# A routed two-layer expert kernel: the first routing round makes its differences ahead on GpSimd, and the first expert begins with halves of its tokens

## The chip, the core and the metric

The kernel is one program on one core of a Trainium2 chip. The metric is the device time of one execution in microseconds (us); a kernel is judged by the median of several executions. Five engines work side by side, each taking its own instructions strictly in their order: PE (TensorE, matmul), DVE (VectorE), ACT (ScalarE), POOL (GpSimd) and SP (here only a queue of DMA issues).

## The reference

```python
def _attn_ref(q, k, v):            # retention: 8 batches, 8 heads, 576 positions, head size 64
    scores = np.matmul(q, k.transpose(0, 1, 3, 2)) / np.sqrt(D_)
    return np.matmul(scores * Dmat, v)          # Dmat: gamma_h ** (i - j), lower triangle
def _moe_ref(x, w_in, w_out):      # 4608 tokens, 512 -> 2048 -> 512
    h = x @ w_in
    return (h - np.tanh(h)) @ w_out
def _moe2_ref(x, w_gate, w1, w2):  # 8 experts of 1024, each takes exactly 576 tokens
    order = np.argsort(-(x @ w_gate).flatten())
    for idx in order:              # best (token, expert) pairs first
        tok, e = idx // E, idx % E
        if assigned[tok] >= 0 or counts[e] >= cap: continue
        assigned[tok] = e; counts[e] += 1
    for e in range(E):
        out[assigned == e] = np.maximum(x[assigned == e] @ w1[e], 0.0) @ w2[e]
```

## The kernel before

Two parts follow each other. In the first (up to about 1043 us) retention and the first pair of layers are computed, and with them the table L of 4608 x 8 gate logits. The change does not touch this part. The second part, `phase_c`, routes tokens and runs the eight experts.

Routing goes in rounds r = 0 to 7; each round fills one expert. All 4608 tokens stand as 128 partitions x 36 columns. A round looks for the threshold of a key: twice ("half" 0 and 1, the upper and the lower 16 bits) it takes three steps of 32, 32 and 64 candidate thresholds. A step compares all keys with all its candidates on DVE (`cmp`, 128 x 36 x 32 or 64), counts with matmuls of the comparison against the proposal table P (`pa`), scales the counts (`ca`), sums them with two small matmuls (`pd`), and finds on DVE the last candidate that still fits (`dm`, `tr`, `pi`). Then come the expert's number `ei` (which lets SP load its weights), running positions, the tables A and R (R in two parts, one of them by ACT), a matmul of the two (`pi`), two small DVE instructions (`im`, `ix`), a last small matmul, and `idx`, the list of the expert's tokens. From `idx` GpSimd gathers 5 tiles of 128 tokens (`xg`).

Only round 0 has nothing to run beside: PE has no other work then. It is "fast": for step 2 GpSimd makes the differences key - threshold ahead (`D`), so that step 2 is one DVE tensor_scalar on D with the two earlier results as per-partition scalars, and not a tensor_tensor.

The rounds 1 to 7, the weight splits (`split_w`: every weight tile is split by ACT into a high part and by POOL into a low part) and the token tiles (`tokens`: 4 PE transposes `tp`, an ACT copy `xh`, a DVE subtraction `xl`) are three Python generators. `experts(r)` writes the matmuls of expert r and after each one or two of them calls `tick`, which advances a clock and lets the generators write their next piece. So the instruction order on every engine is set by that clock and by the numbers behind `yield`, not by readiness on the chip.

An expert has two stages. Stage 1: eight blocks f of 24 matmuls (12 products for each half u of 288 tokens) into two PSUM tiles `ff` of a pool of four; ACT then writes `hh` (relu), and DVE writes `hl` with three instructions that read the same two PSUM tiles. Block f + 2 uses the tiles of block f, so its first matmuls wait until DVE has made `hl` of block f. Stage 2: five output tiles t in the order 0, 4, 1, 2, 3, of 24 matmuls (16 for t = 4, whose parts DVE adds to `o`). The code writes `hl` of block f after the sixth matmul of the next block:

```python
if late and j == 5:
    late.pop()()
```

Of the kernel before, what the change touches and what calls it, by code (L numbers as in the profile page):

```python
# [9 lines left out]
F32 = mybir.dt.float32  # L10
F32R = mybir.dt.float32r
# [16 lines left out]
NCOL = NTOK // 128  # L28
# [687 lines left out]
def phase_c(tc, ctx, w1, w2, rtf, rti, rth, rtb, x2d, L, out):  # L716
# [89 lines left out]
    def route(r):  # L806
# [29 lines left out]
        if r < E - 1:  # L836
# [6 lines left out]
            for half in range(2):  # L843
# [7 lines left out]
                for s, (shift, J) in enumerate(STEPS):  # L851
                    if s == 0:
# [3 lines left out]
                        if fast:  # L856

                            if not half:
                                src = rt([128, NCOL], F32, "hf")
                                nc.gpsimd.tensor_copy(out=src, in_=hi)  # L860
                            D = fp.tile([128, KC, CAP], F32R, tag="xl", name="D", bufs=2)
                            D = D.rearrange("p k t -> p (k t)")[:, :NCOL * 64].bitcast(F32)
                            D = D.rearrange("p (c j) -> p c j", c=NCOL)
# [95 lines left out]
        X72 = X.rearrange("p a c -> p (a c)")  # L959
        nc.tensor.matmul(pt[:, 72:], B["ones"], X72, start=True, stop=True)  # L960
        nc.tensor.matmul(pt[:, :72], B["tri"], X72, start=True, stop=True)
        if r < E - 1:
            se = rt([128, E], F32, "se")
            V.tensor_scalar(se, SB["w8"], mx, None, op0=OP.is_equal)
            V.scalar_tensor_tensor(epen, se, -2 * BIG, epen, op0=OP.mult, op1=OP.add)
            VN[r + 1] = rt([128, NCOL, E], F32, "v")
            V.tensor_tensor(VN[r + 1], L, bc(epen, 1, NCOL), op=OP.min)
        pos = SB["pos"]
        vd = rt([128, 72], F32, "vd")
        pb = rt([128, NCOL], F32, "pb")  # L970
# [23 lines left out]
        if r < E - 1:  # L994

            V.tensor_tensor(SB["hs"], gg[:, :, 0], vd[:, NCOL:], op=OP.add)
            V.scalar_tensor_tensor(tpen, SB["hs"], -2 * BIG, tpen, op0=OP.mult, op1=OP.add)
            V.tensor_tensor(m8, m8, gg[:, :, 0], op=OP.mult)
            V.tensor_tensor(own, own, m8, op=OP.add)
            V.tensor_tensor(rem, rem, nn[:, 0, :], op=OP.subtract)  # L1000
# [10 lines left out]
        if r < E - 1:  # L1011
# [10 lines left out]
    EV, WS, W1, W2, XT, first_done = {}, {}, {}, {}, {}, {}  # L1022

    def load_w1(r):
        EV[r] = nc.sync.value_load(EI[r][:1, :1], min_val=0, max_val=E - 1)
# [29 lines left out]
    def tokens(r):  # L1055
# [17 lines left out]
        for t in range(5):  # L1073
# [4 lines left out]
            h, l = (x[:, :, 128 * t:128 * t + n] for x in (xh, xl))  # L1078
            nc.scalar.activation(h, tp[:, :, :n], AF.Copy)
            V.tensor_tensor(l, tp[:, :, :n], h.bitcast(F32), op=OP.subtract)  # L1080
            yield 1.3
        XT[r] = xh, xl

# [16 lines left out]
                    th_[0] = clock[0] + d * (YS[len(IDX) > 1] if th_ is threads[0] else YS[0])  # L1100

    def experts(r):
        while r not in XT:
            tick(0.2)
        xh, xl = XT.pop(r)
        idx = IDX[r]
        H, late = [], []
        load_w2(r, 0)
        load_w2(r, 1)
        for f in range(8):  # L1110
            load_w2(r, f + 2)
            ps = [psF.tile([128, 512], F32, tag="ff", name="ff")[:, :288] for _ in range(2)]
            while f not in W1:
                tick(0.2)
            w1h, w1l = W1.pop(f)
            prods = [(w, xh, k) for k in range(KC) for w in (w1h, w1l)] + [(w1h, xl, k) for k in range(KC)]
            seq = [(i, u) for i in range(12) for u in range(2)]
            if r == 0 and f == 0:

                seq = [(i, u) for a, b in ((0, 8), (8, 12)) for u in range(2) for i in range(a, b)]  # L1120
            for j, (i, u) in enumerate(seq):
                w, x, k = prods[i]
# [3 lines left out]
                if late and j == 5:  # L1126
                    late.pop()()

            hh = fp.tile([128, CAP + 64], F32R, tag=f"hh{f}", name="hh")
            hl = fp.tile([128, CAP - 64], F32R, tag=f"hl{f}", name="hl")  # L1130
            for u in range(2):
                nc.scalar.activation(hh[:, 288 * u:288 * u + 288], ps[u], AF.Relu)

            def low(ps=ps, hh=hh, hl=hl):
                for a, b, o in ((0, 288, hl[:, :288]), (288, 512, hl[:, 288:]), (512, 576, hh[:, 576:])):
                    V.scalar_tensor_tensor(o, ps[a // 288][:, a % 288:a % 288 + b - a], 0.0, hh[:, a:b].bitcast(F32),  # L1136
                                           op0=OP.max, op1=OP.subtract)
            late.append(low)
            H.append((hh, hl))
            split_w(r, 2, f)  # L1140
            first_done[r] = f == 7
        late.pop()()
        for t in (0, 4, 1, 2, 3):
# [35 lines left out]
    for _ in range(WARM2):  # L1179
        nc.tensor.matmul(warm, B["ones"], tb[:, 256:768], start=True, stop=True)  # L1180

    threads[2][0] = 2.0
    while 0 not in XT:
        tick(0.2)
    for r in range(E):
        experts(r)

# [80 lines left out]
```

## Time and profile before

| what | value |
|---|---|
| times of three runs | 1585.72, 1584.21, 1582.7 us |
| median | 1584.21 us |
| the profiled execution's own time | 1585.81 us, of which the profile's span is 1584.0 us |
| PE busy | 1490.9 us, 94% of the span |
| DVE, ACT, POOL busy | 1131.5, 760.2 and 562.6 us |
| TensorE's granted clock, mean over the span | 0.97 of full speed (2.4 GHz; the lower level is 1.2 GHz) |

Times in the profile count from the start of the span. A matmul's duration is modelled and overlaps the next one's, so pitches (start to start) are used where matmuls follow each other. Brackets at the end of a row tell how long the engine was idle before the instruction, and what it waited for.

### The profile page before, as it was taken

What the parts mean: (1) busy time and instruction counts of PE and PEld (TensorE: products, weight loads), DVE (VectorE), ACT (ScalarE), POOL (GpSimd) and SP (SyncE); (2) the same over time, 40 slices, a digit from 0 to 9 for tenths busy, and PEclk for the clock granted to TensorE, in tenths of its full rate; (3) what the DMA queues carried; (4) which work ended last, traced back from release to release, by engine and by line L of the source; (5) the groups of instructions that cost most, each with busy time, mean ns of one, the idle gap of its engine ahead of it and who ended that gap; (6) DMA issues with size and microseconds to landing.
All of it is one profiled execution on the core that took longest, in us unless ns stands there. A gap on an engine that the chain in (4) does not pass through costs nothing.

```text
span 1584.0 us, 25586 instructions
## 1 busy us (share of the span) xinstructions
PE 1490.9 (94%) x9180; PEld 1291.2 (82%) x9180; DVE 1131.5 (71%) x2772; ACT 760.2 (48%) x1585; POOL 562.6 (36%) x490
## 2 busy tenths in 40 slices
PE   6889998999999999999999999955999999999997
PEld 4678887888888888888888888844887887887996
DVE  6999974878777877777877777867767767766210
ACT  4657873554656454646455556512323323323421
POOL 3546551222213121312221313234545545356542
PEclk7989998999999999999999999976999999999999
DMA  7522220211111111111111100013324324325310
GB/s 255 163 98 80 78 111 21 82 66 41 58 43 49 53 41 61 41 61 41 61 41 42 60 23 20 1 36 112 111 88 137 120 78 136 121 77 190 101 64 30
DMA packets 48607, 122.37 MB, mean 77 GB/s; under 512 B 6624, under 2 KB 13408, under 8 KB 48224
## 3 DMA queue, kind: packets, MB, share of 16 engines
q1 hardware_dynamic: 41184, 99.80, 19.1%
q0 software_dynamic: 6144, 19.93, 3.9%
q8 instruction: 72, 1.18, 0.3%
q10 hardware_dynamic: 1152, 1.02, 0.2%
q14 instruction: 55, 0.45, 0.1%
HBM read 101.85 MB, written 18.87 MB: 76 GB/s over the span
## 4 chain that ended last, share of the span: by engine, by line
PE 76%; DVE 13%; issue 4%; DMA 2%; ACT 2%; POOL 2%; SPq 0%; POOLq 0%; DVEq 0%; ACTq 0%
PE h L394 22%; PE x L457 22%; PE ff L1154 11%; PE ff L1123 10%; PE ps L292 2%; PE ps L339 2%; PE ps L285 2%; PE ps L344 2%; DVE t L418 1%; DVE work L204 1%; PE tp L1077 1%; DVE t L424 1%; DVE work L203 1%; DVE t L420 1%; DVE work L222 1%
## 5 line engine op out<-in xcount | busy, mean ns | idle before, releaser
L438 POOL TENSOR_TENSOR gl<-t,gh 128x384 fp32r<-128x384 f32 x192 | 204.2, 1064 | 664.7 <-ACT gh L435 606.1
L394 PE MATMUL h<-xh,w0h 128*128 128x384 f32 x704 | 239.9, 341 | 3.4 <-DVE t L424 3.3
L404 ACT ACTIVATE S<-h 128x384 f32<-128x384 f32 x192 | 93.7, 488 | 305.7 <-PE h L394 305.4
L394 PE MATMUL h<-xh,w0l 128*128 128x384 f32 x704 | 239.8, 341 | 0.0
L457 PE MATMUL x<-w1h,gh 128*128 128x512 f32 x576 | 235.8, 409 | 2.4 <-ACT gh L435 2.4
L418 DVE SCALAR_TENSOR_TENSOR t<-t,S 128x384 f32<-128x384 f32 x192 | 115.0, 599 | 162.2 <-ACT t L407 161.2
L457 PE MATMUL x<-w1l,gh 128*128 128x512 f32 x576 | 229.5, 398 | 0.0
L457 PE MATMUL x<-w1h,gl 128*128 128x512 f32 x576 | 218.9, 398 | 0.4 <-POOL gl L438 0.4
L498 DVE SCALAR_TENSOR_TENSOR junk<-x2r,wg 128x512 f32<-128x512 f32 x240 | 164.5, 685 | 4.7
L394 PE MATMUL h<-xl,w0h 128*128 128x384 f32 x704 | 153.1, 339 | 0.0
L394 PEld LDWEIGHTS h<-xh,w0h 128*128 128x128 f32 x704 | 133.2, 189 | 13.2 <-DVE t L424 5.5
L1040 POOL TENSOR_TENSOR w2l<-ws,w2h 128x512 fp32r<-128x512 f32 x64 | 82.6, 1292 | 162.9 <-ACT w2h L1039 160.3
L394 PEld LDWEIGHTS h<-xh,w0l 128*128 128x128 f32 x704 | 133.0, 189 | 7.3
L457 PEld LDWEIGHTS x<-w1h,gl 128*128 128x128 f32 x576 | 108.9, 189 | 27.7 <-POOL gl L438 1.5
L1154 PE MATMUL ff<-w2h,hh 128*128 128x512 f32 x320 | 127.6, 399 | 3.0 <-DVE hl L1136 2.0
L424 DVE COPY_PREDICATED t<-m,h 128x384 f32<-128x384 uint16 x192 | 114.8, 598 | 20.4 <-ACT m L413 0.7
L1154 PE MATMUL ff<-w2l,hh 128*128 128x512 f32 (+1 forms) x320 | 127.3, 398 | 0.6 <-POOL w2l L1040 0.6
L407 ACT ACTIVATE t<-S,bias 128x384 f32<-128x384 f32 x192 | 118.3, 616 | 19.0 <-POOL gl L438 3.0
L394 PEld LDWEIGHTS h<-xl,w0h 128*128 128x128 f32 x704 | 126.9, 188 | 0.0
L457 PEld LDWEIGHTS x<-w1h,gh 128*128 128x128 f32 x576 | 109.4, 190 | 20.9 <-ACT gh L435 3.0
L457 PEld LDWEIGHTS x<-w1l,gh 128*128 128x128 f32 x576 | 109.4, 190 | 18.0
L1123 PE MATMUL ff<-xh,w1h 128*128 128x288 f32 x512 | 116.1, 305 | 6.2 <-DVE hl L1136 5.4
(206 smaller groups left out, 3031.3 us busy)
## 6 DMA issues: line engine op xcount, KB each, us to landing
ws<-in_w SPq DMA_DIRECT2D x128, 256.0 KB, 3.6
ain<-in_qkv SPq DMA_DIRECT2D x36, 768.0 KB, 4.2
wst<-in_wio SPq DMA_DIRECT2D x32, 512.0 KB, 3.7
x2d<-x2r SPq DMA_DIRECT2D x33, 256.0 KB, 2.0
w1h<-in_qkv SPq DMA_DIRECT2D x12, 192.0 KB, 3.3
w1l<-in_qkv SPq DMA_DIRECT2D x12, 192.0 KB, 3.4
w0h<-in_qkv SPq DMA_DIRECT2D x12, 192.0 KB, 3.8
w0l<-in_qkv SPq DMA_DIRECT2D x12, 192.0 KB, 4.1
```

The source lines that it names most:

```text
L285: nc.tensor.matmul(PSA[k][a][:, chunk(c)], kt[r, chunk(c)], q[r, chunk(c)], start=True, stop=True)
L394: nc.tensor.matmul(h[:, :TB], w[0][f][:, hp, :], x, start=i == 0, stop=i == 11)
L404: nc.scalar.activation(S, h, AF.Square, scale=KSC)
L407: nc.scalar.activation(AT[s][2], AT[s][1], AF.Square, bias=bias[:, 0:1])
L418: nc.vector.scalar_tensor_tensor(t, t, PA - PB * PB / 4, S, op0=OP.add, op1=OP.mult)
L424: nc.vector.copy_predicated(t, m.bitcast(U16), h)
L438: nc.gpsimd.tensor_tensor(G[s][1], TT.pop(s), G[s][0].bitcast(F32), op=OP.subtract)
L457: nc.tensor.matmul(X2[n][i], g[:, i * 128:i * 128 + 128], w, start=(f == 0 and g is gh and w is wh), stop=(f == NF - 1 and g is gl))
L498: nc.vector.scalar_tensor_tensor(j, r, 1.0, wg[e // 4][:, e % 4, :], op0=OP.mult, op1=OP.mult, accum_out=L[:, c, e:e + 1])
L1040: nc.gpsimd.tensor_tensor(l, s, h.bitcast(F32), op=OP.subtract)
L1123: nc.tensor.matmul(ps[u], w[:, k, :], x[:, k, 288 * u:288 * u + 288], start=i == 0, stop=i == 11)
L1154: nc.tensor.matmul(o, h, w, start=f == 0 and i == 0, stop=f == 7 and i == len(prods) - 1, skip_group_check=t == 4)
```

## The change

Four things are changed, all around round 0 and expert 0.

1. In each half of round 0 GpSimd makes two differences, 32 candidates for step 1 (in the buffers of the token tiles `xh`) and then 64 for step 2 (as before). Step 1 becomes one tensor_scalar on the first of them, in place of a small tensor_scalar (the thresholds) and a tensor_tensor.
2. The next round's values (`se`, `epen`, `v`) are written behind the tables in round 0, and the state update and `best(1)` behind `idx`.
3. Expert 0 starts when three of its five token tiles are there. Its blocks 0 and 1 go together: first the token half u = 0 of both, then u = 1 of both, each with its own ACT relu. Both `hl` come after the sixth matmul of block 2.
4. The routing generator begins at clock 2.0 like the token generator, and the loop that first completed all five tiles is gone.

```diff
-                            D = fp.tile([128, KC, CAP], F32R, tag="xl", name="D", bufs=2)
...
-                            nc.gpsimd.tensor_tensor(D, bc(src, 2, 64), bc(F["s2"], 1, NCOL), op=OP.subtract)
+                            D = []
+                            for i, (n, tag) in enumerate(((32, "xh"), (64, "xl"))):
+                                d = fp.tile([128, KC, CAP], F32R, tag=tag, name="D", bufs=2)
+                                d = d.rearrange("p k t -> p (k t)")[:, :NCOL * n].bitcast(F32)
+                                D.append(d.rearrange("p (c j) -> p c j", c=NCOL))
+                                nc.gpsimd.tensor_tensor(D[i], bc(src, 2, n), bc(F[f"s{i + 1}"], 1, NCOL), op=OP.subtract)
...
+                    elif s == 1 and fast:
+                        cmp_ = rt([128, NCOL, J], BF16, "cmp32")
+                        V.tensor_scalar(cmp_, D[0], pi, None, op0=OP.is_ge)
+                        T = pi
                     elif s == 2 and fast:
                         cmp_ = rt([128, NCOL, J], BF16, "cmp64")
-                        V.tensor_scalar(cmp_, D, T, pi, op0=OP.subtract, op1=OP.is_ge)
+                        V.tensor_scalar(cmp_, D[1], T, pi, op0=OP.subtract, op1=OP.is_ge)
...
+        def values():
...
+                V.tensor_scalar(se, SB["w8"], mx, None, op0=OP.is_equal)
+                V.scalar_tensor_tensor(epen, se, -2 * BIG, epen, op0=OP.mult, op1=OP.add)
+                VN[r + 1] = rt([128, NCOL, E], F32, "v")
+                V.tensor_tensor(VN[r + 1], L, bc(epen, 1, NCOL), op=OP.min)
...
+        if r:
+            values()
...
+        (state if r else values)()
...
-        if r < E - 1:
+        if 0 < r < E - 1:
             best(r + 1)
...
         IDX[r] = idx
+        if r == 0:
+            state()
+            best(1)
...
+            XP[r] = xh, xl, t + 1
...
-        while r not in XT:
+
+        while (XP.get(r, (0, 0, 0))[2] < 3) if r == 0 else r not in XT:
             tick(0.2)
...
+        for fs in ([(0, 1)] if r == 0 else [(0,), (1,)]) + [(f,) for f in range(2, 8)]:
+            load_w2(r, fs[0] + 2)
+            seq = []
+            for f in fs:
...
+                seq += [(u if len(fs) > 1 else 0, f, i, u, ps, *p) for i, p in enumerate(prods) for u in range(2)]
...
+            seq.sort(key=lambda p: p[0])
+            for j, (part, f, i, u, ps, w, x, k) in enumerate(seq):
+                while part and r not in XT:
+                    tick(0.2)
                 nc.tensor.matmul(ps[u], w[:, k, :], x[:, k, 288 * u:288 * u + 288], start=i == 0, stop=i == 11)
...
+                while late and j == 5:
+                    late.pop(0)()
...
-    threads[2][0] = 2.0
-    while 0 not in XT:
-        tick(0.2)
+    threads[0][0] = threads[2][0] = 2.0
```

The change moves instructions on all engines; three places are shown here as the compiled order has them.

On DVE, early in stage 1 of expert 0, before the change: the 64-candidate comparison of round 1 (`cmp64`, in two pieces) and behind it `hl` of block 0, which reads the tiles ff_10873 and ff_10874.

```order
L886 COPY T_10856<-st_10365 128x1
L890 TENSOR_TENSOR cmp64_10854<-hi_10706,st_10365 128x36x32
L1080 TENSOR_TENSOR xl2_10776<-tp_10859,xh2_10775 128x4x64
L903 TENSOR_TENSOR ca_10914<-rt_10895,tf_10357 128x32
L1136 SCALAR_TENSOR_TENSOR hl_10921<-ff_10873,hh_10920 128x288
L1136 SCALAR_TENSOR_TENSOR hl_10921<-ff_10874,hh_10920 128x224
L1136 SCALAR_TENSOR_TENSOR hh_10920<-ff_10874,hh_10920 128x64
```

The same place with the change; ff_10832 and ff_10833 are the PSUM tiles of block 0, and block 2 is to use them again.

```order
L892 COPY T_10911<-st_10365 128x1
L896 TENSOR_TENSOR cmp64_10909<-hi_10708,st_10365 128x36x32 x2
L1160 SCALAR_TENSOR_TENSOR hl_10835<-ff_10832,hh_10834 128x288
L1160 SCALAR_TENSOR_TENSOR hl_10835<-ff_10833,hh_10834 128x224
L1160 SCALAR_TENSOR_TENSOR hh_10834<-ff_10833,hh_10834 128x64
L1160 SCALAR_TENSOR_TENSOR hl_10839<-ff_10836,hh_10838 128x288
```

Before, the small matmuls on PE (L914) that lead to this comparison stood ahead of the first matmul of block 0, so 48 matmuls lay between them and block 2. Now they (L920) stand after the 30th matmul of blocks 0 and 1, and 18 matmuls lie between them and block 2.

On DVE and ACT, in stage 2 of expert 0, before the change: DVE makes round 1's `b1`, the last `hl`, and the tables A and R; ACT makes its part of R ahead of the last block's `hh` and of the split `w2h7`.

```order
L983 TENSOR_TENSOR b1_11362<-st_10365,tf_10357 128x720
L1136 SCALAR_TENSOR_TENSOR hl_11367<-ff_11270,hh_11366 128x288
...
L986 TENSOR_TENSOR A_11361<-st_10365,tf_10357 128x1152
L988 TENSOR_TENSOR R_11363<-b1_11362,st_10365 128x36x20
...
L984 ACTIVATE R_11363<-b1_11362,tf_10357 128x36x20
L1132 ACTIVATE hh_11366<-ff_11270 128x288
...
L1039 ACTIVATE w2h7_11370<-ws2_11157 128x512
L1039 ACTIVATE w1h0_11379<-ws_11306 128x512
```

With the change, first DVE and then ACT: `o_11444` is output tile t = 4, and the `w1h` are splits of the second expert's weights.

```order
L1004 TENSOR_TENSOR b1_11413<-st_10365,tf_10357 128x720
L1188 TENSOR_TENSOR o_11444<-ff_11392,o_11444 64x512
L1007 TENSOR_TENSOR A_11412<-st_10365,tf_10357 128x1152
L1009 TENSOR_TENSOR R_11414<-b1_11413,st_10365 128x36x20
...
L1058 ACTIVATE w2h7_11289<-ws2_11130 128x512
...
L1058 ACTIVATE w1h1_11381<-ws_11357 128x512
L1185 ACTIVATE o_11389<-ff_11296 128x512
L1005 ACTIVATE R_11414<-b1_11413,tf_10357 128x36x20
L1058 ACTIVATE w1h2_11418<-ws_11359 128x512
...
L1058 ACTIVATE w1h4_11438<-ws_11363 128x512
L1187 ACTIVATE o_11444<-ff_11392 64x512
```

On DVE the addition of tile 4 has come between `b1` and A; on ACT its first half stands behind R and five weight splits, and `hh` and `w2h7` no longer stand behind R.

On PE, at the end of expert 0, before the change: `tp_11672` is the last token tile of expert 1, L1154 are matmuls of stage 2, L899 counts round 2's step with 64 candidates, and L1123 are the first matmuls of expert 1.

```order
L1077 MATMUL tp_11672<-tf_10357,xg_11540 128x128 x4
L1154 MATMUL ff_11636<-w2l3_11098,hh_11093 128x512
...
L899 MATMUL rt_11691<-P_11517,cmp64_11651 128x16
...
L1154 MATMUL ff_11636<-w2l7_11371,hh_11366 128x512
L1123 MATMUL ff_11722<-xh2_11563,w1h0_11379 128x288
```

With the change the last three token tiles (`tp`) stand at the end of the stage, the last two directly ahead of expert 1.

```order
L1096 MATMUL tp_11655<-tf_10357,xg_11542 128x128 x4
L1180 MATMUL ff_11577<-w2l7_11290,hh_11237 128x512
...
L920 MATMUL rt_11666<-ca_11652,th_10359 128x32
...
L1096 MATMUL tp_11682<-tf_10357,xg_11557 128x128 x4
L1096 MATMUL tp_11690<-tf_10357,xg_11570 128x128 x4
L1149 MATMUL ff_11703<-xh2_11593,w1h0_11371 128x288
...
L905 MATMUL rt_11719<-P_11548,cmp64_11677 128x16
```

Before, 12 matmuls of stage 2 lay between the last tile and expert 1. Now 12 matmuls of expert 1 lie ahead of L905, which needs both pieces of a `cmp64` that follows from L920.

## Rows read from the trace of the kernel before

**Rows 1.** Busy time by stretch: length, PE, PEld, DVE, ACT, POOL, clock, DMA, GB/s.
```profile
1050.00:1080.00 30.00, 5.83 (x118) 4.54 (x118) 22.03 (x73) 0.00 (x0) 8.40 (x3) 0.50 0.02 5
...
1099.00:1100.00 1.00, 1.00 (x6) 1.00 (x6) 0.86 (x7) 0.00 (x0) 1.00 (x1) 0.50 0.03 8
```

**Rows 2.** Timeline of DVE, step 1 of both halves (start, duration, instruction).
```profile
1055.44 1.35 DVE L890 TENSOR_TENSOR cmp<-hi,st 128x1152 bf16<-128x1152 int32 x1
...
1066.21 1.35 DVE L890 TENSOR_TENSOR cmp<-lf,st 128x1152 bf16<-128x1152 f32 x1
```

**Rows 3.** Timeline of POOL: both differences of round 0, and a weight split.
```profile
1050.56 4.09 POOL L864 TENSOR_TENSOR D<-hf,tf 128x2304 f32<-128x2304 f32 x1 [0.25 <-POOL hf L860]
1062.87 4.09 POOL L864 TENSOR_TENSOR D<-lf,tf 128x2304 f32<-128x2304 f32 x1 [8.21 <-DVE lf L848]
...
1105.56 1.29 POOL L1040 TENSOR_TENSOR w2l<-ws,w2h 128x512 fp32r<-128x512 f32 x1 [5.49 <-ACT w2h L1039]
```

**Rows 4.** Timelines of POOL and DVE at 45 us; then all of line 203.
```profile
45.47 1.46 POOL L233 TENSOR_TENSOR w0l<-work,w0h 128x512 fp32r<-128x512 f32 x1 [1.97 <-ACT w0h L227]
...
45.72 1.49 DVE L203 TENSOR_SCALAR work<-wst,ci 128x512 int32<-128x512 int32 x1
...
L203 DVE TENSOR_SCALAR work<-wst,ci x22: 527/544/1623, 9.2 to 202.8; 128x512 int32<-128x512 int32 x22
```

**Rows 5.** Timelines, end of round 0: from the expert's number to its token list.
```profile
1077.12 0.14 DVE L955 TENSOR_SCALAR ei<-mx 128x1 int32<-128x1 f32 x1
...
1081.17 1.30 ACT L1039 ACTIVATE w1h<-ws 128x512 fp32r<-128x512 f32 x2 [32.87 <-DMA ws<-in_w]
...
1083.31 1.36 PE L992 MATMUL rt<-R,A 128*128 128x160 bf16 x9 [5.75 <-ACT R L984]
...
1083.20 0.20 DVE L996 TENSOR_TENSOR st<-st,vd 128x36 f32<-128x36 f32 x1
...
1086.01 0.16 DVE L1015 TENSOR_REDUCE idx<-rt 128x5 int32<-128x10 f32 x1
```

**Rows 6.** Timelines, from the token list to block 2 of expert 0.
```profile
1085.68 6.07 PE L1180 MATMUL warm<-tb 128*128 128x512 bf16 x14
...
1089.81 0.46 DVE L828 TENSOR_TENSOR P<-st,m 128x288 bf16<-128x288 f32 x1
...
1093.20 0.69 DVE L1080 TENSOR_TENSOR xl<-tp,xh 128x512 fp32r<-128x512 f32 x1 [1.00 <-ACT xh L1079]
...
1098.13 0.38 PE L1123 MATMUL ff<-xh,w1h 128*128 128x288 f32 x1
...
1107.71 0.43 PE L1123 MATMUL ff<-xh,w1h 128*128 128x288 f32 x2
```

**Rows 7.** A routing step in expert 1 on PE and DVE; waits of PE, 1290 to 1350.
```profile
1176.31 0.19 PE L914 MATMUL rt<-ca,th 128*128 128x32 f16 x1
...
1177.92 2.61 DVE L890 TENSOR_TENSOR cmp<-lf,st 128x1152 bf16<-128x1152 f32 x2
1180.44 0.75 DVE L1136 SCALAR_TENSOR_TENSOR hl<-ff,hh 128x288 fp32r<-128x288 f32 x2
...
PE ff L1123 <- DVE hl L1136: 2.6, 3, 2.0
```

**Rows 8.** Waits of PE, 1098 to 1166 (total, times, longest); stage 2 of expert 0.
```profile
PE tp L1077 <- DMA xg<-x2d,idx: 1.1, 2, 0.7
PE ff L1154 <- ACT w2h L1039: 1.0, 1, 1.0
...
PE ff L1154 <- POOL w2l L1040: 0.6, 1, 0.6
...
1141.98 0.68 DVE L1162 TENSOR_TENSOR o<-ff,o 64x512 f32<-64x512 f32 x1 [2.17 <-ACT o L1161]
...
1128.99 0.48 PE L1154 MATMUL ff<-w2h,hh 128*128 128x512 f32 x1
...
1133.64 0.39 PE L1154 MATMUL ff<-w2l,hh 128*128 128x512 f32 x1
```

More of the change, by code (lines that the diff above doesn't have):

```diff
@@ L961, in route, with state @@
         nc.tensor.matmul(pt[:, :72], B["tri"], X72, start=True, stop=True)
-        if r < E - 1:
[L963 to L967, printed above, removed]
+        def values():
+            if r < E - 1:
+                se = rt([128, E], F32, "se")
+                V.tensor_scalar(se, SB["w8"], mx, None, op0=OP.is_equal)
+                V.scalar_tensor_tensor(epen, se, -2 * BIG, epen, op0=OP.mult, op1=OP.add)
+                VN[r + 1] = rt([128, NCOL, E], F32, "v")
+                V.tensor_tensor(VN[r + 1], L, bc(epen, 1, NCOL), op=OP.min)
+        def state():
+            if r < E - 1:
+                V.tensor_tensor(SB["hs"], gg[:, :, 0], vd[:, NCOL:], op=OP.add)
+                V.scalar_tensor_tensor(tpen, SB["hs"], -2 * BIG, tpen, op0=OP.mult, op1=OP.add)
+                V.tensor_tensor(m8, m8, gg[:, :, 0], op=OP.mult)
+                V.tensor_tensor(own, own, m8, op=OP.add)
+                V.tensor_tensor(rem, rem, nn[:, 0, :], op=OP.subtract)
+        if r:
+            values()
         pos = SB["pos"]
@@ L993, in route @@
                              R[:, 4 * g:4 * g + 4].rearrange("p c a t -> p (c a t)"), start=g == 0, stop=g == 8)
[L994 to L1000, printed above, removed]
+        (state if r else values)()
         im = rt([128, 4, 40], F32, "im")
@@ L1010, in route @@
             nc.tensor.matmul(pj, B["sq"][:, 128 * q:128 * q + 128], ixq[:, q], start=q == 0, stop=q == 3)
-        if r < E - 1:
+        if 0 < r < E - 1:
             best(r + 1)
@@ L1020, in route @@
             yield 2.9
-    EV, WS, W1, W2, XT, first_done = {}, {}, {}, {}, {}, {}
+    EV, WS, W1, W2, XT, XP, first_done = {}, {}, {}, {}, {}, {}, {}
     def load_w1(r):
@@ L1102, in experts @@
     def experts(r):
-        while r not in XT:
+        while (XP.get(r, (0, 0, 0))[2] < 3) if r == 0 else r not in XT:
             tick(0.2)
-        xh, xl = XT.pop(r)
+        xh, xl, _ = XP[r]
         idx = IDX[r]
@@ L1109, in experts @@
         load_w2(r, 1)
[L1110 to L1113, printed above, removed]
-                tick(0.2)
[L1115 to L1122, printed above, removed]
+        for fs in ([(0, 1)] if r == 0 else [(0,), (1,)]) + [(f,) for f in range(2, 8)]:
+            load_w2(r, fs[0] + 2)
+            seq = []
+            for f in fs:
+                ps = [psF.tile([128, 512], F32, tag="ff", name="ff")[:, :288] for _ in range(2)]
+                while f not in W1:
+                    tick(0.2)
+                w1h, w1l = W1.pop(f)
+                prods = [(w, xh, k) for k in range(KC) for w in (w1h, w1l)] + [(w1h, xl, k) for k in range(KC)]
+                seq += [(u if len(fs) > 1 else 0, f, i, u, ps, *p) for i, p in enumerate(prods) for u in range(2)]
+                hh = fp.tile([128, CAP + 64], F32R, tag=f"hh{f}", name="hh")
+                hl = fp.tile([128, CAP - 64], F32R, tag=f"hl{f}", name="hl")
+                H.append((hh, hl))
+            seq.sort(key=lambda p: p[0])
+            for j, (part, f, i, u, ps, w, x, k) in enumerate(seq):
+                while part and r not in XT:
+                    tick(0.2)
                 nc.tensor.matmul(ps[u], w[:, k, :], x[:, k, 288 * u:288 * u + 288], start=i == 0, stop=i == 11)
@@ L1125, in experts, with low @@
                     tick(TK1)
[L1126 to L1140, printed above, removed]
+                while late and j == 5:
+                    late.pop(0)()
+                if i == 11:
+                    hh, hl = H[f]
+                    nc.scalar.activation(hh[:, 288 * u:288 * u + 288], ps[u], AF.Relu)
+                    if u == 1:
+                        def low(ps=ps, hh=hh, hl=hl):
+                            for a, b, o in ((0, 288, hl[:, :288]), (288, 512, hl[:, 288:]), (512, 576, hh[:, 576:])):
+                                V.scalar_tensor_tensor(o, ps[a // 288][:, a % 288:a % 288 + b - a], 0.0,
+                                                       hh[:, a:b].bitcast(F32), op0=OP.max, op1=OP.subtract)
+                        late.append(low)
+            for f in fs:
+                split_w(r, 2, f)
+                if len(fs) > 1 and f == 0:
+                    load_w2(r, 3)
             first_done[r] = f == 7
@@ L1180, in phase_c @@
         nc.tensor.matmul(warm, B["ones"], tb[:, 256:768], start=True, stop=True)
-    threads[2][0] = 2.0
-    while 0 not in XT:
-        tick(0.2)
+    threads[0][0] = threads[2][0] = 2.0
     for r in range(E):
```

2 lines of the change are left out of this document (removed).

## The prediction

> **What bounds the kernel now.** I read the busy times by stretch first. From 1050 to 1080 us PE works 5.8 of 30 us and DVE 22 [rows 1]: round 0 runs alone, and each microsecond of its chain is a microsecond of the kernel. After it PE is close to always busy, so from the first expert on a time counts only where PE waits; the waits of PE show how few those are now [rows 8]. So I follow three things: when round 0 delivers its token list, when PE starts block 2 of expert 0, and which waits of PE come and go until expert 1 starts.
>
> **Step 1 on differences.** A half now needs two differences on POOL ahead of step 2. The one with 64 candidates takes 4.09; a weight split of 512 elements takes 1.29 [rows 3]. The one with 32 (1152 elements) then takes between 2.05 (half of 4.09) and 2.29 (on the line through both); with 2.17 the pair takes 6.26. It starts at 1050.56, as the single one did, and ends at 1056.82.
>
> Step 1's new tensor_scalar is asked for at about 1055.1, in the middle of the second difference. Can it run then? The trace has the case: a POOL subtraction runs from 45.47 to 46.93, and a DVE tensor_scalar of 512 elements that begins at 45.72 ends at 47.21, 0.28 after it, though its like takes 0.53 to 0.54 when nothing is in its way and up to 1.62 otherwise [rows 4]. I read it as held until POOL's instruction is over, with 0.28 per 512 elements still to do, 0.63 for 1152. So step 1 ends at 1056.82 + 0.63 = 1057.45, where the old comparison ended at 1055.44 + 1.35 = 1056.79 [rows 2]: 0.66 later. In half 1 the differences start at 1062.87 + 0.66 [rows 3], end at 1069.79, and step 1 ends at 1070.42; the old one ended at 1067.56 [rows 2]. Round 0 is **2.86 later** (2.6 to 3.1 with the bounds of the pair). The second difference is then done when step 2 comes, so nothing more is lost there.
>
> The Trainium skill (SBUF — State Buffer, section "Who interferes with whom") states that a VectorE tensor_scalar in its two-port mode and a GpSimd instruction exclude each other for a whole instruction, whoever starts first. By it the compare would also run its full length after the hold, an estimate of 0.2 more in each half; the row has the shorter rest, and I keep the row.
>
> **Values, state, `best`.** Moving the three `v` instructions away from the positions frees up to 0.8 on DVE, but the matmul of the tables at 1083.31 waits for ACT's part of R [rows 5]. That stands on ACT behind two weight splits, which begin when the weights land, 4.05 after `ei` (1077.12 to 1081.17) [rows 5], and `ei` gains nothing. I count 0 (at best 0.8, were ACT not last). `idx` then ends at 1086.17 + 2.86 = 1089.0. Seven instructions now stand between it and round 1's keys, five adds of 0.2 [rows 5] and `best` with one reduction of about twice that: 1.7 in all.
>
> **From the list to block 2.** P of round 1 ended at 1090.27 [rows 6] and now ends 2.86 + 1.7 later, at 1094.8. The 14 warming matmuls, at 1085.68 + 6.07 [rows 6], end 2.86 later too, at 1094.6. DVE is now the queue that decides: four small instructions (0.65), two `xl` (0.69 each [rows 6]), a `ca` (0.2), six small ones (1.2), a comparison (1.35 [rows 2]) and the third `xl`: 1100.3. Block 0 can use `xl` only then; its first matmul comes at about 1098, as before (1098.13), so the early start buys nearly nothing. From 1100.3 PE has 22 matmuls at 0.148 (144 of them, with the routing between, lie between 1107.71 [rows 6] and 1128.99 [rows 8]), two transposes and a count, 4.5 together: L920 at 1104.8. Then DVE: from such a matmul to the `hl` behind two comparisons it took 4.13 (1176.31 to 1180.44), and half of 0.75 for the first `hl` [rows 7]. Block 2's first matmuls start at 1109.3 and 1109.7, 1.8 after the 1107.71 of before. Bounds: 1.3 if the matmuls keep the pitch without routing, 4.3 if the clock stays at 0.50 as at 1099 [rows 1] for half of them.
>
> **The same collision in blocks 4 and 7.** There one comparison stands ahead of the `hl` (4.13 less 1.26 = 2.87, and 0.4 for `hl`). PE has 18 and 20 matmuls of cover, 2.7 and 3.0: waits of 0.9 and 0.5, with the second tile's counted. That this kind of wait is real, one of 2.0 shows [rows 7].
>
> **Stage 2, tables of round 1.** Count from the stage's first matmul, S; its pitch is 0.2325 (20 between 1128.99 and 1133.64 [rows 8]). PE asks for X, made just ahead of `ei`, at its 25th matmul: S + 5.8. Weights land 4.05 later, S + 9.9; then ACT: two splits (1.3 [rows 5]), tile 0's copy (0.65), R (0.9), three splits (2.0), tile 4 (0.65): S + 15.4. DVE adds tile 4 (0.68 [rows 8]) and only then makes A (1.35) and R (0.9): S + 18.2. PE wants the tables at its 55th matmul, with the routing between at S + 13.3. A wait of **4.8** (3 to 5.5). Already in before DVE stood 2.17 waiting for ACT's tile 4 [rows 8], but behind the tables.
>
> **What goes.** PE no longer waits 1.0 and 0.6 for `w2h` and `w2l` [rows 8], since R no longer stands ahead of them; and it comes later to the gathered tokens, so 1.1 [rows 8] goes.
>
> **Expert 1's start.** After the last matmul of stage 2: 1.2 until the third `xl`, 1.36 small ones, two comparisons with an `xl` between (3.2): 5.8 until L905, less two transposes and 12 matmuls, 2.8. A wait of 3.0 (1.5 to 3.5).
>
> **Sum:** 1.8 + 1.4 + 4.8 - 2.7 + 3.0 = **+8.3**. The profiled execution would take 1585.8 + 8.3 = 1594.1; it lay 1.6 above the median of 1584.2, so the median becomes **1592.5**. The rounds of experts 1 to 5 come 5 to 14 matmuls later in the order, past other `hl`; the waits of 2.6 in one expert [rows 7] may shrink there and appear elsewhere. I take 0, bounds -2.5 and +2.5. A measurement of this kernel can tell about 0.2%, 3.2 us, from no change.
>
> **Rivals.**
> - *The compare is not held* (its form, float to bf16 with one scalar, is not that of the row). Each step 1 is then some 0.7 shorter; the second difference of half 1 (done at 1068.4) is the next thing late, so round 0 is 1.0 earlier instead of 2.86 later: 1588.6. For it: no row has just this form. Against it: the row's instruction is alike. 0.12.
> - *The clock falls after the long waits.* After a stretch with little on PE the clock was 0.50 at 1099, with 6 matmuls in 1 us [rows 1]. If it falls again in stage 2, 3.4 us of matmuls at half pace add 1.7, twice that if it lasts: 1595.5. 0.13.
> - *No long wait at the tables.* If round 1's `ei` comes early enough, or the weights land as fast as ACT asks, 4.8 goes to 1 or less: 1588, and with shorter waits of the other kinds down to 1586. 0.12; half of it within 0.2%.
> - *The halves pay in full (faster).* Place: DVE between the list and block 2. If `xl` and `hl` come before PE needs them, PE runs from the third tile without a pause: two tiles earlier (2.5), 16 matmuls no longer at the low clock (1.8), the old waits (2.7) gone, against 2.86: -4.1, 1580.1. It decides itself at block 2: below 1104 it holds. Against it: the two comparisons stand ahead of `hl` in DVE's order. 0.06.
>
> **Numbers.** The forecast, with its bounds, has 0.57: 1589 to 1596. The range reaches down to the third rival and up past the second: 1586 to 1598. Slower: 0.57, the clock's 0.13, 0.07 of the case that is not held (the later rounds can bring it under 0.2%) and 0.05 of the third: 0.82. Same 0.12, faster 0.06.
>
> **What the changed profile would show.** Two tensor_scalar on D that end about 0.6 after POOL's second difference; `idx` at 1089 (not held: at 1085); block 2 of expert 0 waiting about 2 for `hl`; the matmul of A and R in stage 2 waiting about 5 for DVE, with DVE waiting for ACT's tile 4; and L905 waiting some 3 at expert 1. If the compare runs through the difference, or if DVE reaches the tables in time, the prediction is wrong by that term.

## The result, and the profile after

The median went from 1583.45 us (four executions, 1582.48 to 1585.72) to **1598.47 us** (four, 1597.32 to 1600.9): ratio 1.0096, 95% interval 1.0080 to 1.0112, so 12.7 to 17.8 us slower. The forecast of 1592.5 had the direction; the time lies 0.5 above its range. The execution with the profile took 1598.27 us (span 1596.5, granted clock 0.966). Its first difference starts 0.86 earlier than that of before [rows 3], in a part that is not changed; I add 0.86 to each comparison of a time with before.

Timelines of POOL, DVE and PE, after: round 0, the start of block 2, and the tables of round 1 (start, duration, engine, line; in brackets the idle time ahead and what ended it).

```profile
1049.70 6.21 POOL L866 TENSOR_TENSOR D<-hf,tf 128x1152 f32<-128x1152 f32 x2 [0.25 <-POOL hf L860]
...
1062.60 6.21 POOL L866 TENSOR_TENSOR D<-lf,tf 128x1152 f32<-128x1152 f32 x2 [6.69 <-DVE lf L848]
...
1054.36 2.16 DVE L875 TENSOR_SCALAR cmp<-D,pi 128x1152 bf16<-128x1152 f32 x1
...
1065.73 3.70 DVE L875 TENSOR_SCALAR cmp<-D,pi 128x1152 bf16<-128x1152 f32 x1
...
1085.24 1.36 PE L1013 MATMUL rt<-R,A 128*128 128x160 bf16 x9 [5.81 <-ACT R L1005]
...
1087.79 0.17 DVE L1031 TENSOR_REDUCE idx<-rt 128x5 int32<-128x10 f32 x1 [0.37 <-PE rt L1026]
...
1109.55 0.89 PE L1149 MATMUL ff<-xh,w1h 128*128 128x288 f32 x2 [1.92 <-DVE hl L1160]
...
1149.41 0.68 DVE L1188 TENSOR_TENSOR o<-ff,o 64x512 f32<-64x512 f32 x1 [5.45 <-ACT o L1187]
1150.02 1.34 DVE L1007 TENSOR_TENSOR A<-st,tf 128x1152 bf16<-128x1152 int32 x1
1151.28 0.89 DVE L1009 TENSOR_TENSOR R<-b,st 128x720 bf16<-128x720 bf16 x1
...
1152.23 1.38 PE L1013 MATMUL rt<-R,A 128*128 128x160 bf16 x9 [4.48 <-DVE R L1009]
```

The compare ends at 1056.52 and 1069.43, 0.61 and 0.62 behind POOL's second difference (1055.91, 1068.81): it was held, and had the shorter rest of [rows 4] left (forecast 0.63). The list comes at 1087.79, 2.64 later than in [rows 5]; the matmul that ends the wait there still waits for ACT. Block 2 starts 2.70 later than in [rows 6], behind `hl`. At the tables DVE stands 5.45 for ACT's tile 4 and PE 4.48 for DVE; 4.8 was forecast for PE.

Waits of PE, after, from 1089.1 to 1213.3 (total, times, longest); [rows 8] has those of before, but ends at 1166:

```profile
PE rt L1013 <- DVE R L1009: 4.5, 1, 4.5
PE ff L1149 <- DVE hl L1160: 3.2, 3, 1.9
PE rt L905 <- DVE cmp L896: 1.6, 1, 1.6
PE ff L1149 <- DVE xl L1099: 1.3, 1, 1.3
PE ff L1149 <- ACT xh L1098: 1.0, 2, 0.7
PE tp L1096 <- DVE xl L1099: 0.6, 1, 0.6
PE ff L1180 <- POOL w2l L1059: 0.6, 1, 0.6
...
PE ff L1180 <- ACT w2h L1058: 0.4, 1, 0.4
...
```

Busy time by stretch, columns as in [rows 1] (the clock is the third number from the end): in expert 0 ahead of block 2, behind the wait at the tables, and at the start of expert 1:

```profile
1099.00:1103.00 4.00, 3.87 (x18) 3.86 (x19) 0.77 (x2) 0.90 (x2) 2.84 (x3) 0.57 0.00 0
1152.00:1157.00 5.00, 4.77 (x18) 4.00 (x19) 2.38 (x10) 0.00 (x0) 3.70 (x5) 0.50 0.14 30
1177.00:1181.00 4.00, 4.00 (x23) 3.86 (x24) 1.05 (x6) 1.23 (x3) 0.48 (x1) 0.58 0.02 4
```

After the waits of 4.5 and 1.6 the clock is at its lower level: 5 us at 0.50 lose 2.5, 4 us at 0.58 lose 1.7. The first stretch, which loses 1.7 too, is at the lower level in both kernels ([rows 1] has a part of it in before), but the forecast counted the matmuls there at full pace. The other two have no such clock in before, which has one of its own later:

```profile
1313.00:1317.00 4.00, 3.49 (x14) 3.29 (x15) 3.75 (x8) 1.91 (x5) 2.52 (x2) 0.57 0.81 288
```

Expert 1's first output tile and the last of all, on ACT, before and then after:

```profile
1199.80 0.60 ACT L1159 ACTIVATE o<-ff 128x512 f32<-128x512 f32 x1 [2.81 <-issue]
...
1574.77 0.60 ACT L1159 ACTIVATE o<-ff 128x512 f32<-128x512 f32 x1 [4.79 <-PE ff L1154]
```

```profile
1213.33 0.60 ACT L1185 ACTIVATE o<-ff 128x512 f32<-128x512 f32 x1
...
1587.24 0.60 ACT L1185 ACTIVATE o<-ff 128x512 f32<-128x512 f32 x1 [4.79 <-PE ff L1180]
```

So 14.4 are lost by expert 1's first output, and 13.3 at the end: before loses 1.7 at 1313, and after does not.

The forecast's terms beside what the traces show:

| step | forecast | measured in the traces |
|---|---|---|
| block 2 of expert 0, list of round 0 included | +1.8 | +2.70 |
| blocks 4 and 7 | +1.4 | +1.3 (3.2 less block 2's 1.9) |
| tables of round 1 | +4.8 | +4.5 |
| waits that go | -2.7 | -1.7 (waits for `w2h` and `w2l` of 1.0 together come back in expert 1) |
| expert 1's start | +3.0 | +2.5 (1.6, 0.6, and 0.3 for `xh`) |
| a wait of before for `hl` ahead of expert 1's second stage, which goes | 0 | -1.1 |
| low clock behind the new waits | 0 | +4.2 |
| sum, until expert 1's output | +8.3 | +12.4 of 14.4 |

The 1.1 is this wait of before; expert 1's second stage has none like it after:

```profile
1193.28 0.50 PE L1154 MATMUL ff<-w2h,hh 128*128 128x512 f32 x1 [1.09 <-DVE hl L1136]
```

What fills the last 2.0 is not shown.

### The profile page after: what moved, and what is told of

Its sections match the earlier page's. It is cut to its first block, busy times and chain, and to the rows that moved or that the text cites. A ratio compares the mean times of both kernels' runs of the same rounds, so it can differ in the third digit from the quotient of the medians.

```text
span 1596.5 us, 25586 instructions
## 1 busy us (share of the span) xinstructions
PE 1494.6 (94%) x9180; PEld 1293.6 (81%) x9180; DVE 1133.7 (71%) x2770; ACT 760.6 (48%) x1585; POOL 566.3 (35%) x492
## 3 DMA queue, kind: packets, MB, share of 16 engines
q10 hardware_dynamic: 1152, 1.02, 0.2%
## 4 chain that ended last, share of the span: by engine, by line
PE 73%; DVE 15%; issue 4%; ACT 3%; DMA 3%; POOL 1%; POOLq 0%; SPq 0%; ACTq 0%; DVEq 0%
PE h L394 22%; PE x L457 22%; PE ff L1180 10%; PE ff L1149 9%; PE ps L292 2%; PE ps L339 2%; PE ps L285 2%; PE ps L344 2%; DVE t L418 1%; PE tp L1096 1%; DMA wst<-in_wio 1%; DVE work L204 1%; DVE t L424 1%; DVE work L203 1%; DVE work L222 1%
```

## The experiments

Each has its own executions of the kernel before on the same chip; "us" is the ratio less 1, times 1585. Where one run is set against another, the difference is that of their "us", and its uncertainty holds both intervals.

| run | what | ratio (95%) | us |
|---|---|---|---|
| - | the change | 1.0096 (1.0080 to 1.0112) | +15.2 |
| e1 | before, with the differences alone | 1.0019 (1.0010 to 1.0028) | +3.0 |
| e2 | the change, old differences | 1.0083 (1.0069 to 1.0098) | +13.2 |
| e3 | the change, tables' wait filled | 1.0098 (1.0083 to 1.0113) | +15.5 |
| e4 | the change, tile 4 third | 1.0095 (1.0081 to 1.0109) | +15.1 |
| e5 | e4, five weight splits behind the gathers | 1.0099 (1.0084 to 1.0115) | +15.7 |
| e6 | the change, `hl` ahead | 1.0092 (1.0076 to 1.0107) | +14.6 |
| e7 | the change, routing earlier | 1.0039 (1.0026 to 1.0053) | +6.2 |
| e8 | e7, old differences | 1.0007 (0.9997 to 1.0017) | +1.1 |
| e9 | e4, stores behind the gathers | 1.0047 (1.0034 to 1.0060) | +7.4 |
| e10 | the change, wait at expert 1 filled | 1.0092 (1.0079 to 1.0105) | +14.6 |
| e11 | e8, stores behind the gathers | 1.0002 (0.9993 to 1.0011) | +0.3 |
| e12 | before, stores behind the gathers | 0.9994 (0.9986 to 1.0003) | -1.0 |
| e13 | the change, stores behind the gathers | 1.0072 (1.0059 to 1.0085) | +11.4 |
| e14 | e13, tables' wait filled | 1.0076 (1.0061 to 1.0090) | +12.0 |
| e15 | e11, tile 4 third | 0.9968 (0.9956 to 0.9980) | -5.1 |
| e16 | e9, `hl` ahead | 1.0028 (1.0018 to 1.0039) | +4.4 |
| e17 | e12, tile 4 third | 0.9989 (0.9980 to 0.9998) | -1.7 |
| e18 | e15, new differences | 1.0008 (0.9999 to 1.0017) | +1.3 |

**Round 0 by itself (e1, e2).** e1 puts the two differences and the new step 1, as in the diff above, into the kernel before; e2 takes them out of the change.

> The kernel before with the two differences and the new step 1 of round 0 alone; order of everything else as before. Theory (the compare is held until POOL's second difference ends): +2.7 us, 1586.2, both tensor_scalar on D end about 0.61 after POOL. Rival (held only by chance, or the hold hidden by other work of round 0): -1 to 0 us.

> The changed kernel with the single difference and the old step 1; values behind the tables and the halves of tokens stay. Theory (the two parts add up): 2.7 us less than the changed kernel, 1595.8, that is some 12 above the kernel before, all of it behind the list of round 0. Rival (the late list is what causes the waits in the first expert and in stage 2): near the kernel before, 1584 to 1588.

+3.0 and -2.0, the second with some 3 either way: the held compare costs what was forecast. Counted from the first difference, the list of round 0 comes 2.68 later in e1 than in before, and 2.75 earlier in e2 than with the change. In e2, where the values and the state stand behind the tables as in the change, it comes within 0.1 of before. Both compares of e1, and its step 2, which has 2304 elements and nothing in its way:

```profile
1056.21 2.16 DVE L875 TENSOR_SCALAR cmp<-D,pi 128x1152 bf16<-128x1152 f32 x1
1060.20 1.48 DVE L879 TENSOR_SCALAR cmp<-D,pi 128x2304 bf16<-128x2304 f32 x1
...
1067.59 3.69 DVE L875 TENSOR_SCALAR cmp<-D,pi 128x1152 bf16<-128x1152 f32 x1
```

**The wait at the tables (e3, e4, e5, e9).** e3 fills it, e4 takes it away:

```diff
+        for _ in range(60 if r == 1 else 0):            # e3
+            nc.tensor.matmul(pi, B["ones"], tb[:, 256:416], start=True, stop=True)
-        for t in (0, 4, 1, 2, 3):                       # e4
+        for t in ((0, 1, 4, 2, 3) if r == 0 else (0, 4, 1, 2, 3)):
```

> The changed kernel with 60 matmuls of 160 columns, of no use to the result, in the wait ahead of the tables of round 1 (about 4 us at full clock, in a wait of 4.5). Theory (the clock falls in that wait, and the nine table matmuls and the nine of stage 2 behind it run at half pace): granted clock 1.00 from 1152 to 1157, and 2 to 2.3 us less than the changed kernel, 1596.3. Rival (the slow matmuls behind the wait have another cause, as their weight loads): the same time as the changed kernel, 1598.5, or more by what of the 60 sticks out of the wait.

> The changed kernel with the output tiles of expert 0 in the order 0, 1, 4, 2, 3 in place of 0, 4, 1, 2, 3, so that DVE makes A and R ahead of the addition of tile 4. Theory (the wait of 4.5 at the tables is that addition, and the slow clock behind it follows from the wait): wait below 1, no low clock near 1152, 4.5 + 2.2 = 6.7 less than the changed kernel, 1591.8. Rival (the splits on ACT are next late, R's second half waits for them): a wait of 3 or more stays at the tables, 1597 or more.

Neither gave any time. In e3 the clock stayed up behind the wait, but fell earlier, in expert 0 (windows):

```profile
1108.00:1112.00 4.00, 3.87 (x17) 3.62 (x18) 1.06 (x5) 0.00 (x0) 1.51 (x2) 0.57 0.48 131
1146.00:1151.00 5.00, 5.00 (x60) 4.57 (x59) 1.54 (x2) 4.89 (x9) 4.82 (x5) 1.00 0.99 348
1151.00:1157.00 6.00, 5.42 (x41) 4.37 (x39) 4.45 (x16) 0.60 (x1) 3.04 (x3) 1.00 0.25 81
```

The list of round 1 comes 1.5 earlier than with the change (counted from the first difference), and yet the gathers behind it start 2.3 later, at 1161.20. In e4 the wait at the tables is gone, but another has come (a window, then a wait of PE):

```profile
1099.00:1107.00 8.00, 7.08 (x42) 6.84 (x42) 2.17 (x5) 1.69 (x4) 2.98 (x3) 0.57 0.00 1
...
PE tp L1096 <- DMA xg<-x2d,idx: 3.5, 1, 3.5
```

The window explains a part of e4's result: its clock stays low longer in expert 0 than with the change, and again from 1113 to 1117, so its second stage begins 3.1 later (counted from the first difference), ahead of the place of the edit. From there to expert 1's first matmul it takes 37.3, with the change 38.4: 1.2 are gained of 6.7. In that stretch expert 1's gathered tokens are next late. I took POOL's weight splits for the cause:

```diff
         for f in range(8):
+            while r == 1 and f > 2 and r not in XP:     # e5, on e4
+                yield 0.2
             split_w(r, 1, f)
```

> The run with tile 4 third, and beside it five of the eight splits of expert 1's first weights written behind the gathers of its tokens, so that POOL reaches the gathers as soon as the list of round 1 is there. Theory (once the tables come in time, the gathers on POOL, behind eight splits and a store that waits for tile 4, set the start of expert 1: the wait of 3.5 for the gathered tokens): that wait goes to 0.5 or less with the low clock behind it, 4 to 5.5 us less than with tile 4 third alone, +9.5 to +11 to the kernel before. Rival (round 2's comparisons, or the late splits, are next late at once): a wait of 3 or more at L905 or for w1, and +14 to +15.

That theory fell: the wait is 3.4, and the time is unchanged. The timelines of POOL and DVE in e5 show why:

```profile
1150.46 1.01 POOL L1191 DMA_INDIRECT out<-o,idx  x1 [0.15 <-issue]
...
1157.65 1.00 POOL L1191 DMA_INDIRECT out<-o,idx  x1 [4.84 <-DMA out<-o,idx]
1161.17 0.90 POOL L1191 DMA_INDIRECT out<-o,idx  x1 [2.52 <-DMA out<-o,idx]
1162.38 0.98 POOL L1083 DMA_INDIRECT xg<-x2d,idx  x1 [0.30 <-DVE tr L930]
...
1155.38 0.16 DVE L1031 TENSOR_REDUCE idx<-rt 128x5 int32<-128x10 f32 x1
```

The list is there at 1155.5; the gathers (`xg`) start at 1162.4, because two stores of expert 0 stand ahead of them, and the trace has each released by the landing of a store before it. e9 writes these stores behind the gathers:

```diff
-            nc.gpsimd.indirect_dma_start(out=out, ...)
+            if r == 0 and t in (1, 4) and 1 not in XG: stores.append(store)   # e9, on e4
+            else: store()                               # tokens(1) writes them behind its last gather
```

> The run with tile 4 third, and beside it expert 0's stores of tiles 1 and 4 written behind the gathers of expert 1's tokens on POOL. Theory (with the tables in time, each store on POOL waits until the store ahead of it has landed, and the gathers stand behind two such waits: 4.8 and 2.5 in the run with the gathers first): the gathers start within 1 us of the list of round 1, PE's wait of 3.5 for them and the low clock behind it go, 3.5 to 5.5 less than with tile 4 third, +9.5 to +11.5 to the kernel before. Rival (DVE's comparisons of round 2 or the free o buffers are next late): +13 to +15.

7.6 less than e4, where 3.5 to 5.5 were forecast. The gathers start at 1156.06, the stores wait behind them, and PE's wait for `xg` falls to 0.3 (DVE, then POOL, e9):

```profile
1152.51 0.16 DVE L1031 TENSOR_REDUCE idx<-rt 128x5 int32<-128x10 f32 x1
...
1148.36 7.54 POOL L1060 TENSOR_TENSOR w1l<-ws,w1h 128x512 fp32r<-128x512 f32 x6
1156.06 0.97 POOL L1082 DMA_INDIRECT xg<-x2d,idx  x1 [0.16 <-issue]
...
1162.35 1.01 POOL L1195 DMA_INDIRECT out<-o,idx  x1 [0.30 <-issue]
1165.93 0.91 POOL L1195 DMA_INDIRECT out<-o,idx  x1 [2.58 <-DMA out<-o,idx]
```

The gathers follow the list by 3.4 and not by the forecast 1, because six weight splits now stand ahead of them on POOL. From the first matmul of stage 2 to that of expert 1 e9 takes 32.4, 4.9 less than e4, which is within the forecast. Another 3.2 between the two traces lie ahead of stage 2, where the edit moves nothing and e4's clock is lower; so only the 4.9 are shown to be the stores'.

**Low clock (e10, e13, e14).** e10 is e3's edit with 24 matmuls ahead of L905 in round 2; e13 puts e9's edit on the change, e14 adds e3's to it.

> The changed kernel with 24 matmuls of 160 columns, of no use to the result, in the wait of 1.6 at the start of expert 1 (ahead of L905, round 2's candidates of 64). Theory (the low clock from 1177 to 1181 follows from that wait and costs 1.7 because nothing else is late behind it): granted clock 1.00 there, 1.5 to 2 less than the changed kernel, +13.3 to the kernel before. Rival (the clock falls anyway, for the waits ahead of that one, or its loss comes back at the next wait): +14.5 to +15.5.

> The changed kernel with expert 0's stores of tiles 4 and 1 behind the gathers of expert 1 and nothing else. Theory (the stores decide only once the tables come in time; here the list comes late and the gathers follow it by 1.4): 0 to 1 less than the changed kernel, +14 to +15 to the kernel before, wait of 4.5 at the tables and low clock behind it as there. Rival (the stores alone are the cause): +7 to +10.

> The run with the stores behind the gathers, and beside it the 60 matmuls without use in the wait ahead of the tables. Theory (low clock behind a wait is paid when nothing else is late): clock 1.00 at 1152 to 1157, the list 1.5 earlier, 1.5 to 2.5 less than with the stores behind the gathers alone. Rival (the loss at low clock is never on the path): no difference.

In e10 the clock stays up at expert 1, and falls at another place (windows):

```profile
1172.00:1180.00 8.00, 7.91 (x86) 7.61 (x87) 5.53 (x15) 1.27 (x4) 1.05 (x1) 1.00 0.09 35
1385.00:1388.00 3.00, 3.00 (x15) 3.00 (x14) 2.93 (x8) 0.59 (x2) 2.07 (x2) 0.52 0.99 351
```

The times of e10, and of e14 against e13, show no gain, and e13 is between its two theories (its interval meets the change's). e14's executions go from 1592.29 at a mean clock of 0.972 to 1600.87 at 0.965. The profiled one is the fastest, and from 1104 on the clock does not fall in it. In e13's profiled one it falls at 1150, 1177 and 1467, which loses 6.8, and its last output comes 5.4 later, counted from the first difference. From stage 2's first matmul to expert 1's e14 takes 36.7 and e13 38.4, the 1.5 to 2.5 of the theory. So between these two executions the low clock is paid for in good part; but the fill does not keep it from falling elsewhere in the other executions, and the price of a single stretch stays open.

**Block 2's wait (e6, e16).** The `hl` of blocks 0 and 1 are made by halves, two ahead of the `cmp64` and one between its pieces.

```diff
-                    if u == 1:
+                    if u == 1 or len(fs) > 1:           # low() then makes the pieces of this u alone
-                while late and j == 5:
+                while late and j in ((5,) if len(fs) == 1 else (26, 37)):
```

> The changed kernel with the hl of blocks 0 and 1 of expert 0 written by halves, the first halves ahead of the two cmp64 and the next between them, so that block 2's PSUM tiles come free sooner. Theory A (the waits of PE add up, as the prediction's sum has it): block 2's wait of 1.9 goes to 0.5 or less, and the time falls by 1.4 to 1.9, +13.2 to the kernel before. Theory B (up to expert 1 the chain of round 1 through DVE, ACT and POOL decides, and a wait taken away ahead of the tables comes back at them): the wait goes, the tables' wait of 4.5 grows by as much, +15.

> The run with tile 4 third and the stores behind the gathers (+7.4 to the kernel before), and beside it the hl of blocks 0 and 1 by halves ahead of and between the two cmp64. Theory A (with the later chain cleared a wait of PE is paid in full): block 2's wait of 1.9 goes to 0.5 or less and the time falls by 1.4 to 1.9. Theory B (round 1's own chain through DVE still decides, and the hl delay it by 0.4): 0 to +0.5 more.

On the change it looks more like theory B: the waits for `hl` fall from 3.2 to 1.3 and the tables' wait grows by 0.6 (e6), a third of what went, and the time moves by 0.6, within its interval.

```profile
PE rt L1013 <- DVE R L1009: 5.1, 1, 5.1
...
PE ff L1149 <- DVE hl L1160: 1.3, 2, 0.9
```

With the later places cleared (e16 against e9) 3.0 are gained. In the traces 3.8 are gained by stage 2's first matmul, and all of it is kept to expert 1's: 2.2 of waits for `hl`, and the rest where e9's clock is 0.57 from 1109 to 1113 and e16's is not. The intervals of the times just meet, so theory A is likely and its size open.

**The place of the routing (e7, e8, e11, e15, e17, e18).** The change lets the routing begin 2.0 later against the matmuls (`threads[0][0] = threads[2][0] = 2.0`) and expert 0 two tiles earlier. Of the 304 matmuls of expert 0, so many are written ahead of round 1's instructions:

| | before | change | e7 |
|---|---|---|---|
| X (L960, L966) | 192 | 217 | 206 |
| tables (L992, L1013) | 222 | 247 | 236 |

```diff
-    threads[0][0] = threads[2][0] = 2.0
+    threads[2][0] = 2.0                                 # e7; e8 with the old differences
```

> The changed kernel with the routing written 2.0 earlier against the matmuls, as in the kernel before (some 16 matmuls of the first expert). Theory (the place of round 1 in the order makes the waits at the tables and at expert 1's start): gathers behind six splits in place of eight, tables' wait under 3, 3 to 6 us less than the changed kernel, +9 to +12 to the kernel before. Rival (the first expert's start has too little PE work to cover DVE wherever the routing stands): the same waits ahead of block 2 and earlier, +14 to +16.

> The run with the routing written earlier, with the single difference and the old step 1 in round 0. Theory (round 0 adds to the rest): 2 to 2.9 us less than the run with the routing written earlier alone. Rival (the later list is what makes the waits behind it): 4 or more less.

9.0 of the 15.2 go with this one number, more than the 3 to 6 forecast. In e7's trace PE waits neither for `hl` nor for R from 1090 to 1180; 2.8 are left behind the tables. With the old differences what is left can't be told from no change. e8 is 5.1 below e7 (2.4 to 7.7 by both intervals), so that round 0's 3.0 alone can make it; its traces differ by 3.0. On e8 the stores and tile 4 follow; e12 and e17 are the same two edits without the halves.

> The run with the routing written earlier and the old differences, and beside it the stores of tiles 1 and 4 of expert 0 behind the gathers of expert 1. Theory (there too the gathers wait 3.8 for the stores, from the list at 1146.3 to 1150.2): tokens of expert 1 come 1 to 3 us earlier, 0 to 2 less than without, -1 to +1 to the kernel before. Rival (DVE's xl are what its tiles wait for, 1.4): no difference.

> The kernel before with its stores of tiles 1 and 4 of expert 0 behind the gathers of expert 1. Theory (gathers start 4.6 after the list because a store ahead of them waits, and PE waits 1.1 for them): that wait goes, 1 us less than the kernel before. Rival: round 2 on DVE is next late, no difference.

> The run with the routing written earlier, old differences and stores behind the gathers, and beside it the output tiles of expert 0 in the order 0, 1, 4, 2, 3. Theory (there DVE stands 5.7 for ACT's half of tile 4 ahead of the products of the tables, and PE then waits 3.1): that wait goes, 2 to 3 less, -2 to -3 to the kernel before. Rival (ACT's half of R or the gathers are next late): -1 to +1.

> The kernel before with its stores of tiles 1 and 4 of expert 0 behind the gathers and the output tiles of expert 0 in the order 0, 1, 4, 2, 3, without halves of tokens. Theory (the halves give a part of the 5: they let the first expert begin ahead of its last two tiles): -1 to -2 to the kernel before, the run with the halves stays 3 to 4 faster than this one. Rival (stores and tile 4 make all of it): -4 to -5.

> The run with the routing written earlier, stores behind the gathers and tile 4 third, and beside it the pair of differences and the new step 1 of round 0. Theory (the held compare costs 2.7 to 3 wherever it stands, since round 0 runs alone): 2.5 to 3.5 more than with the old differences, -2 to the kernel before. Rival (the pair moves the routing against the first expert, and waits come or go with it): less than 1 or more than 5.

e11's profile has the addition of tile 4 ahead of the products of the tables, on DVE, and PE waiting behind it:

```profile
1142.15 0.68 DVE L1187 TENSOR_TENSOR o<-ff,o 64x512 f32<-64x512 f32 x1 [5.71 <-ACT o L1186]
...
1144.46 0.26 PE L1020 MATMUL rt<-ix,tb 128*128 128x10 bf16 x4 [3.12 <-DVE ix L1015]
```

The stores alone give nothing that can be told from no change (e11 against e8, and e12). In e15 the wait behind tile 4 is gone; the longest waits of PE from 1090 to 1180:

```profile
PE ff L1148 <- ACT xh L1097: 1.1, 2, 0.7
PE tp L1095 <- DVE xl L1098: 1.0, 1, 1.0
PE ff L1148 <- DVE xl L1098: 0.4, 1, 0.4
...
```

**e15 beats both kernels**: 1581.57 us against 1586.24 of before on its chip. It is 5.4 below e11, where 2 to 3 were forecast; in the traces 2.7 of that are there at expert 1's first output. Without the halves the two edits give 1.7 (e17), so what the change keeps beside them in e15 gives some 3.4 of the 5.1 (1.0 to 5.8 by both intervals). That is the halves of tokens, and with them the moved values and state, which bring the list only 0.2 earlier in the traces. The differences take this back: e18 is 6.4 above e15 (4.0 to 8.8 by both intervals), which by its median is the rival's "more than 5" and by its interval reaches the theory too. Its traces differ by 3.4, and its mean clock is 0.968 against 0.970, so a part of the 6.4 is likely clock.

## Where the prediction was right, and where it failed

*Right:* the held compare (0.63 against 0.61 and 0.62; round 0 +2.86 against +2.64 in the trace and +3.0 in e1); values and state at nothing (e2's list); the places of the waits for `hl`, at the tables and at expert 1, and most of their sizes (L905 waited 1.6, the low end of its bounds). The Trainium skill (SBUF — State Buffer, section "Who interferes with whom") has the exclusive hold, and the trace agrees. By it the compare would have its full length still to go, an estimate of 0.74 here (half of the 1.48 above); the runs have 0.61 to 0.62, and the measurement decides.

*Failed:* the step that failed is the pace of the matmuls behind each new wait. The sum counted them at full pace (0.2325 in stage 2), and had the fall of the clock as a rival at one place ("3.4 us of matmuls at half pace add 1.7", 0.13) and not as a term. The clock fell behind two of the waits, 4.2 in the trace. Block 2 was 0.9 too little for the same reason: `xl` came at the forecast time, but from there to L920 PE took 5.8 in place of 4.5, with 1.7 lost at a clock of 0.57. The forecast had this in its bounds only.

"What goes" was another 1.0 too much, because waits for `w2h` and `w2l` came back in expert 1's second stage. These make 6.1 of what was missing, and the smaller waits take 2.0 of it back (the 1.1 for `hl` among them); 2.0 of the 14.4 stay unexplained. Of the 15.2 of the medians the traces show 13.3; the rest is within the interval.

*Right in the places, not as prices of a repair:* each term was a wait of PE, but behind some of them stand others that end almost as late. Without the tables' wait the stores hold up the gathers (e4, e9), and on the change block 2's wait gives no time that can be told (e6). What made most of the loss was one thing, which the prediction saw in the order but did not price as such: round 1 stands 25 matmuls later in expert 0. Moved 11 back, 9.0 are gone (e7), and with the old differences as well 14.1 (e8).

*Rivals:* a compare that is not held, and no long wait at the tables, are refuted by the rows above. "The clock falls after the long waits" came true in the trace, and at one place more than it named. "The halves pay in full" was refuted for the change, but the halves do pay, some 3.4, once the order lets them (e15, e17).

## What to carry over

A sum of waits of one engine found the places of a slowdown and about half its size (8.3 of 15.2), but it says little on what a repair gives: look for what is late next, queues of stores on a DMA-issuing engine too. When a stage is begun earlier against a side chain that runs beside it, count how many matmuls the chain's instructions have moved, and move the chain as well. Price a fall of the clock behind each new wait as a term, and before a run is called without effect, look where its clock fell.

## What was unexpected of the hardware

- Executions of one kernel differ by the clock. Over 72 executions of the kernel before, beside e1 to e16, the mean granted clock goes from 0.966 to 0.973 and the time from 1587.95 to 1582.09 (the ends of the clock), on a line 1.08 us for 0.001. As 0.001 of 1585 us is 1.6 us, an estimate is that two thirds of what a low clock takes from PE show in the time. The four of the change have 0.965 to 0.967, against 0.969 in the mean; an estimate from that line puts some 3 of the 15.2 on the clock.
- Where the clock is low changes with small edits far away: filling a wait at 1176 kept it up there, and it fell at 1385 (e10); filling the wait at the tables kept it up at 1152, and it fell at 1108 (e3).
- A store by indices waited 2.5 to 4.8 us on POOL, released in the trace by the landing of a store ahead of it (e5, e9), with all that is queued behind it. Whether the chip or the program asks for this order is not shown.
